# Attention and bilinear FFN on one core: the first batch's loads in phases, and five output transposes moved from TensorE to DMA

## The chip, the core and the metric

The kernel runs on one core of a Trainium2 chip. The metric is device time in microseconds (us) of one execution. Engines are named as the profile names them: PE is TensorE (matrix products and transposes), DVE is VectorE, ACT is ScalarE, POOL is GpSimd, SP is SyncE. DMAs are issued by a queue of SP or ACT ("hardware" queues in the profile) or by POOL ("software"); the profile counts the time of all of them against the same 16 DMA engines.

## The reference, cut to what matters

```python
B, H, S, D = 8, 8, 576, 64               # batches, heads, sequence, head size
scores = q @ k.transpose(0, 1, 3, 2) / sqrt(D) + bias_table[bucket(|i - j|)]   # 32 buckets per head
attn   = softmax(scores)
x      = (attn @ v)  -> (B*S, H*D) = (4608, 512)
out    = ((x @ w_a) * (x @ w_b)) @ w_out        # w_a, w_b: 512 x 1536, w_out: 1536 x 512
```

All inputs and the output are float32. The kernel takes its products of bfloat16 tiles, with float32 sums in PSUM; only the first transposes, of pairs 0 to 2 and of the first tails, read float32.

## The kernel before

The kernel works on 32 pairs of heads, four pairs to a batch. For each pair it multiplies q by k (`qk`), takes the exponential on ACT (`ex`, tile `at`), multiplies by the exponential of the bias on DVE (`mul`, tile `W`), multiplies by the values on PE (`av`), divides on DVE (`norm`, tile `XG`), and transposes the result into `xn` (`t_x`), the input of the FFN. From pair 4 on, FFN units (`pa`, `pb`, `po`) of an earlier batch are woven between the steps of attention, and PE is then the limit. Pairs 0 to 3 have no FFN work beside them. I call the stretch from the start to pair 8 the ramp.

The order of instructions is fixed by the program, and in the timelines here the sync queue issues its DMAs in that order.

The loads of the first batch (cuts marked with `...`):

```python
load32(0, q, q32, (nc.sync, nc.sync));  load32(0, k, k32, (nc.scalar, nc.scalar))
load32(1, q, q32, (nc.sync, nc.sync));  load32(1, k, k32, (nc.sync, nc.sync))
...
load_pad(nc.sync, k, kt32, 0, 1)        # last 64 rows of k ("tails"), float32
load_pad(nc.sync, q, qt32, 0, 1)
...
pad(nc.gpsimd, vt[0][:, 0:4, :, :], Dh + 1)     # memsets of zero padding on POOL
ones(nc.gpsimd, vt[0][:, 0:4, :, :])
...
nc.sync.dma_start(out=tab.ap(), in_=tab_sb[0:H, :])   # exp(bias) table to DRAM, W is read from it
load32(2, q, q32, (nc.sync, nc.sync))
load32(2, k, k32, (nc.sync, nc.sync))
load_w(nc.sync, 0)
...                                     # Wt
load_w(nc.sync, 1)

load_vp(0, 0)                           # software loads from here: values of pair 0
load_vt(0, 1)                           # value tails of batch 0
load_p(q, qn, 0, 3);  load_p(k, kn, 0, 3)
load_vp(0, 1)
load_t(v, None, 0, 4, 8)                # values of heads 4 to 7
load_w_in(0)
...                                     # pads, tails, q and k of batch 1, w_a and w_b
```

The output of a pair. `XG` has two buffers, so pair p + 2 writes what pair p's transpose reads:

```python
XG = [wpool.tile([128, 5, 2, Dh], BF16, name=f"XG{i}") for i in range(2)]
XD = 8
def t_x(p, where=None):
    xg = XG[p % 2]
    if XD <= p < NP - 1:                # by DMA, on the sync queue
        nc.sync.dma_start_transpose(out=xn_sb[hp][:, main]..., in_=xg[:, 0:4, :, :]...)
        nc.sync.dma_start_transpose(out=xn_sb[hp][:, rest]..., in_=xg[0:64, 4, :, :]...)
        return
    ps = bank(where, BF16, f"trx{p}")   # else five transposes on PE; c_x copies them out of PSUM
    for jq in range(5):
        nc.tensor.transpose(ps[:, 128 * jq:128 * jq + 128], xg[:, jq, :, :], ident)
```

The transposes of q and k of batch 2 (`QTb`, `KTb`, and the tails `QTt`, `KTt`) are DMA transposes too and go by the same sync queue (`turns`), one in each of steps 5, 6 and 7. Their sources, the last parts of `w_a` and `w_b`, and the whole of `w_out` are software loads issued at step 2:

```python
if s == 2:
    load_w_in(3);  load_w_in(4);  load_w_in(5)
    load_t(q, qn, 2, 0, 8);  load_t(k, kn, 2, 0, 8)
    ...
    load_tails(2, 2)
    load_w_out()                        # one load of 1,536 KB, tile wo
...
# steps 5 to 31
if s > XD:
    steps += [lambda: t_x(s - 1), lambda: turns(s)]
...
if s <= XD:
    steps += [lambda: t_x(s - 1, TR), lambda: c_x(s - 1), lambda: turns(s)]
```

The softmax here doesn't subtract the row's maximum and nothing guards it: scores larger than these inputs give would overflow.

## Time and profile before

The time before is 433.4 us, the median of 3 runs (432.4 to 433.4). The profiled execution spans 432.3 us; that execution took 434.11 us, more than the timed runs of its round, so a delta against it flatters the other kernel by about 0.7 us.

| from the profile of before | value |
|---|---|
| PE busy over the span | 411.5 us, 95% |
| PE busy, 100 to 400 us | 297.84 of 300 us |
| PE clock granted, 10.4 to 13.5 and 13.5 to 21.6 us | 0.72 and 0.50 |
| first `av` product with the main values on PE | 21.6 us |
| first FFN product leaves PSUM (`ha`) | 39.85 us |
| exponential of pair 8 starts | 82.29 us |

The window view of before shows where time can be won. Columns: stretch and its length, busy time of each engine with instruction counts, PE's granted clock, DMA share (time of the packets over the time of 16 engines; above 1 where packets overlap), GB/s. The engines stand in the order PE, PE's weight loads, DVE, ACT, POOL.

```profile
10.40:13.50 3.10, 0.38 (x1) 0.16 (x2) 0.38 (x1) 1.25 (x2) 2.89 (x5) 0.72 2.26 153
13.50:21.60 8.10, 6.88 (x30) 3.61 (x31) 2.53 (x8) 4.50 (x6) 7.51 (x13) 0.50 1.69 200
83.00:90.00 7.00, 6.84 (x81) 4.17 (x80) 3.39 (x9) 4.79 (x7) 6.02 (x8) 1.00 2.38 171
100.00:400.00 300.00, 297.84 (x2347) 144.94 (x2384) 133.54 (x313) 172.39 (x246) 42.89 (x52) 1.00 0.77 80
```

The last row says that PE has nothing to gain after 100 us except by doing less. In the first row PE works 0.38 of 3.1 us, and in the second its clock is at half: the short idle stretch is paid twice. The Trainium skill, "TensorE: Matmul & The Clock Gate", Part 1, puts the fall to half after an idle window of about 3.4 us. The trace agrees that half clock goes with a gap, but not on its length: PE's longest idle pieces here are 1.32 and 1.45 us, and a mean clock of 0.72 over 10.4 to 13.5 us puts the fall (1.00 to 0.50) at about 11.8 us, when PE had been idle since 10.37.

What PE and DVE wait for at the start, from the waits view of before (columns: total us, times, longest us):

```profile
PE trt L556 <- DMA qt<-in_q_dram: 1.5, 1, 1.5
PE trt L556 <- DMA kt<-in_k_dram: 1.3, 1, 1.3
DVE at L358 <- DMA W<-bias_tab: 4.2, 1, 4.2
```

And the chain that ended last, in order of time (start us, length us, what), has the same load in it:

```profile
1.17 3.97 DMA k<-in_k_dram
7.27 6.10 DMA qt<-in_q_dram
13.51 0.89 PE trt L556 x3
```

So the last of the float32 tails (of q) arrives at 13.4 us, after 6.1 us under way, and PE stands still for the tails of k and of q. Later in the ramp, the sync queue of before issues the batch-2 transposes with nothing between them (timeline view of SP; start us, time in the queue, what):

```profile
54.81 3.78 SPq L331 DMA_TRANSPOSE QTb<-qn  x1
58.77 9.02 SPq L331 DMA_TRANSPOSE KTb<-kn  x1
67.95 1.51 SPq L326 DMA_TRANSPOSE QTt<-qtl  x1
69.58 2.52 SPq L326 DMA_TRANSPOSE KTt<-ktl  x1
```

### The profile page before, as it was taken

To read this page: it belongs to the slowest core of one execution; us is meant where nothing else is said; L and a number is where in the kernel's file an instruction comes from. 1 tells how busy PE (TensorE), PEld (TensorE's weight loads), DVE (VectorE), ACT (ScalarE), POOL (GpSimd) and SP (SyncE) were. 2 spreads that over 40 slices of the span, in tenths; PEclk is the share of its full clock that TensorE was granted. 3 is DMA by queue.
4 is the path that set the end of the run, shared out by engine and by line. 5 is a ranking of instruction groups with operands and counts; after the bars stand their busy time and mean duration, and the time that the engine had idled before them with its cause. 6 is when DMAs were issued, how large, how long until landed. Compare 5 with 4: busy or idle time off the path is not lost.

```text
span 432.3 us, 8313 instructions
## 1 busy us (share of the span) xinstructions
PE 411.5 (95%) x3296; PEld 204.4 (47%) x3350; DVE 195.9 (45%) x482; ACT 241.4 (56%) x340; POOL 118.1 (27%) x164
## 2 busy tenths in 40 slices
PE   6688898999999999999999999999999999999995
PEld 2355444554445544444444454544444454444442
DVE  4295556545553455245634553355435541321320
ACT  4484766666665766666656675666566633223321
POOL 8989792583008100930073003000000000000000
PEclk9599999999999999999999999999999999999999
DMA  9999999999909990999099908931021002002004
GB/s 152 191 181 164 181 170 177 144 161 153 107 15 128 165 129 14 107 185 141 15 76 185 159 16 52 177 71 27 21 80 39 15 23 78 0 11 87 0 2 97
DMA packets 174055, 42.13 MB, mean 97 GB/s; under 512 B 160568, under 2 KB 169408, under 8 KB 174016
## 3 DMA queue, kind: packets, MB, share of 16 engines
q0 software_dynamic: 113296, 17.97, 67.4%
q1 hardware_dynamic: 59520, 23.27, 30.6%
q8 instruction: 26, 0.43, 0.4%
q10 hardware_dynamic: 1200, 0.36, 0.4%
q14 instruction: 13, 0.11, 0.1%
HBM read 38.83 MB, written 9.45 MB: 112 GB/s over the span
## 4 chain that ended last, share of the span: by engine, by line
PE 90%; DVE 3%; DMA 2%; ACT 2%; issue 1%; SPq 0%; ACTq 0%; DVEq 0%
PE pb L474 23%; PE po L484 22%; PE pa L464 21%; PE av L409 9%; PE qk L339 7%; PE av L400 2%; PE qkt L364 2%; PE qkt L367 1%; DMA qt<-in_q_dram 1%; DMA k<-in_k_dram 1%; DVE XG L418 1%; ACT at L350 1%; DVE at L358 1%; DVE g L477 1%; PE qktt L370 0%
## 5 line engine op out<-in xcount | busy, mean ns | idle before, releaser
L350 ACT ACTIVATE at<-qk 128x1024 bf16<-128x1024 f32 x128 | 125.9, 1024 | 23.5 <-PE qk L339 23.5
L477 DVE TENSOR_TENSOR g<-pb,ha 128x512 bf16<-128x512 f32 x108 | 74.7, 692 | 126.0 <-PE pb L474 102.7
L464 PE MATMUL pa<-xn,wa 128*128 128x512 bf16 x415 | 109.8, 379 | 0.8
L474 PE MATMUL pb<-xn,wb 128*128 128x512 bf16 x414 | 109.4, 379 | 1.0 <-DVE g L477 0.2
L468 ACT ACTIVATE ha<-pa 128x512 f32<-128x512 f32 x108 | 64.6, 598 | 77.2 <-PE pa L464 75.1
L484 PE MATMUL po<-wo,g 128*128 128x512 bf16 x416 | 99.6, 379 | 1.0 <-issue 0.2
L358 DVE TENSOR_TENSOR at<-at,W 128x512 bf16<-128x512 bf16 (+1 forms) x128 | 60.2, 483 | 14.2 <-ACT at L350 10.0
L474 PEld LDWEIGHTS <-wb 128*128 128x128 bf16 x432 | 38.6, 97 | 53.1 <-issue 18.0
L464 PEld LDWEIGHTS <-wa 128*128 128x128 bf16 x432 | 38.8, 98 | 49.3 <-issue 10.3
L484 PEld LDWEIGHTS <-g 128*128 128x128 bf16 x432 | 38.5, 98 | 46.1 <-issue 7.6
L488 ACT ACTIVATE ob<-po 128x512 f32<-128x512 f32 x36 | 21.5, 597 | 69.0 <-PE po L484 69.0
L124 POOL DMA_DIRECT2D vm<-in_v_dram x32 | 27.6, 876 | 112.0 <-PE av L409 111.8
L409 PE MATMUL av<-vm,at 128*128 128x65 bf16 x1024 | 47.3, 194 | 0.0
L409 PEld LDWEIGHTS <-at 128*128 128x128 bf16 x1024 | 42.7, 98 | 6.7
L417 DVE RECIPROCAL rc<-av 128x6 f32<-128x6 f32 x64 | 12.1, 188 | 53.4 <-PE av L409 53.4
L400 PE MATMUL av<-vt,att 128*128 128x130 bf16 x160 | 35.2, 220 | 0.1
L418 DVE TENSOR_TENSOR XG<-av,rc 128x384 bf16<-128x384 f32 x64 | 31.4, 491 | 2.9 <-DVE rc L417 0.8
L378 ACT ACTIVATE att<-qkt 128x1024 bf16<-128x1024 f32 x32 | 32.7, 1021 | 0.0
L339 PE MATMUL qk<-QTb,KTb 64*128 64x512 bf16 x192 | 29.1, 381 | 0.0
L124 POOL DMA_DIRECT2D qn<-in_q_dram x28 | 24.8, 914 | 12.9 <-PE qk L339 5.8
L124 POOL DMA_DIRECT2D kn<-in_k_dram x28 | 24.7, 900 | 13.0 <-DMA vt<-in_v_dram 4.6
L400 PEld LDWEIGHTS <-att 128*128 128x128 bf16 x160 | 15.8, 99 | 7.3 <-issue 0.7
(98 smaller groups left out, 214.5 us busy)
## 6 DMA issues: line engine op xcount, KB each, us to landing
out_dram<-ob SPq DMA_DIRECT2D x32, 256.0 KB, 4.3
qn<-in_q_dram POOLq DMA_DIRECT2D x28, 128.0 KB, 9.5
kn<-in_k_dram POOLq DMA_DIRECT2D x28, 128.0 KB, 13.1
vm<-in_v_dram POOLq DMA_DIRECT2D x28, 128.0 KB, 6.0
wa<-in_moe_w_a_dram POOLq DMA_DIRECT2D x6, 256.0 KB, 7.5
wb<-in_moe_w_b_dram POOLq DMA_DIRECT2D x6, 256.0 KB, 8.1
wo<-in_moe_w_out_dram POOLq DMA_DIRECT2D x1, 1536.0 KB, 15.4
out_dram<-ob SPq DMA_DIRECT2D x8, 128.0 KB, 2.3
```

Source lines behind the costliest of these rows:

```text
L124: nc.gpsimd.dma_start(out=(vm[b % 2][:, h0:h1, t, 0:Dh] if dst is None else dst[b % 2][:, :].rearrange("p (t h d) -> p t h d", h=H, t=NM)[ ...
L339: nc.tensor.matmul(out=ps[:, hh, :], lhsT=kT_(p, t)[r, :], rhs=qT[r, :, :], start=True, stop=True)
L350: nc.scalar.activation(out=at[:, :, :], in_=ps[:, :, :], func=ACTF.Exp, scale=scale)
L358: nc.vector.tensor_tensor(out=at[:, :, lo:hi], in0=at[:, :, lo:hi], in1=w[:, :, y:(None if z < 0 else z):-1], op=MULT)
L400: nc.tensor.matmul(out=pav[:, slot, :, :], lhsT=x, rhs=vt[b // 2 % 2][:, 4 * i + hp, :, :], start=True, stop=True)
L409: nc.tensor.matmul(out=pav[:, slot, hh, :], lhsT=x, rhs=vm[i][:, 2 * hp + hh, t, :], start=False, stop=True, skip_group_check=True)
L418: nc.vector.tensor_tensor(out=xg[:, j0:j0 + n, :, :], in0=pav[:, 0:n, :, 0:Dh], in1=rc.unsqueeze(3).to_broadcast([128, n, 2, Dh]), op=MULT)
L464: nc.tensor.matmul(out=pa[:, :], lhsT=wa_sb[df // FW][:, mc, 128 * (df % FW):128 * (df % FW) + 128], rhs=xn_sb[mc][:, xin(c)], start=(mc = ...
L468: nc.scalar.activation(out=ha[:, :], in_=pa[:, :], func=ACTF.Copy)
L474: nc.tensor.matmul(out=pb[:, :], lhsT=wb_sb[df // FW][:, mc, 128 * (df % FW):128 * (df % FW) + 128], rhs=xn_sb[mc][:, xin(c)], start=(mc = ...
L477: nc.vector.tensor_tensor(out=g_sb[df][:, :], in0=pb[:, :], in1=ff["ha"][:, :], op=MULT)
L484: nc.tensor.matmul(out=po[:, :], lhsT=g_sb[df][:, 128 * tt:128 * tt + 128], rhs=wo_sb[:, df, :], start=(df == 0), stop=(df == NDF - 1))
```

## The change

The intent has two halves. First, the loads of batch 0 come in phases: POOL does all its pads before its first value load, so that the float32 loads of the hardware queues have the DMA engines to themselves, and the values then come in a few large software loads. The loads of pair 2's keys move behind those of `W`. Second, the outputs of pairs 0, 1 and 4 to 6 are transposed by DMA as those from pair 8 on already were, which takes 25 transposes from PE and their copies from DVE.

```diff
-    load_pad(nc.sync, k, kt32, 0, 1)
+    load_pad(nc.scalar, k, kt32, 0, 1)
...
-    pad(nc.gpsimd, vt[0][:, 0:4, :, :], Dh + 1)
-    ones(nc.gpsimd, vt[0][:, 0:4, :, :])
     for i in range(2):
...
+        pad(nc.gpsimd, vt[i], Dh + 1)
+        ones(nc.gpsimd, vt[i])
+        for x in (ktl, qtl):
+            pad(nc.gpsimd, x[i], Dh)          # the later pads of these tiles are taken away
...
-    warm_up(1)
+    warm_up(2)
...
     load32(2, q, q32, (nc.sync, nc.sync))
-    load32(2, k, k32, (nc.sync, nc.sync))
     load_w(nc.sync, 0)
     ...                                       # Wt
+    load32(2, k, k32, (nc.sync, nc.sync))
     load_w(nc.sync, 1)
 
-    load_vp(0, 0)
+    load_v(0)                                 # all 8 heads, four loads
     load_vt(0, 1)
     load_p(q, qn, 0, 3)
     load_p(k, kn, 0, 3)
-    load_vp(0, 1)
-    load_t(v, None, 0, 4, 8)
...
-    XD = 8
+    XD = {0, 1, 4, 5, 6} | set(range(8, NP - 1))
...
-        if XD <= p < NP - 1:
+        if p in XD:
...                                            # in the loop of pairs 0 to 3
-        if s > 1:
-            t_x(s - 2, FF)
...
-        if s > 1:
-            c_x(s - 2)
...
-            tails_next(s + 1, 1, None)
+            tails_next(s + 1, 1, ACT)
...
+        if s in (1, 2):
+            t_x(s - 1)
...                                            # pairs 5 to 31
-            if s > XD:
+            if s - 1 in XD:
                 steps += [lambda: t_x(s - 1), lambda: turns(s)]
```

The second `warm_up` product is one more that PE does without use before the first transposes. Two more moves are cut: `av(s - 1, 4)` goes ahead of `mul(s, 2)`, and the copy of pair 2's output goes to ACT. Where pair 4 to 6's outputs go by DMA, their transposes are now put into the sync queue ahead of the batch-2 transposes of the same step.

More of the change, by code (lines that the diff above doesn't have):

```diff
@@ L235 @@
     load_p(k, kn, 0, 3)
-    load_vp(0, 1)
-    load_t(v, None, 0, 4, 8)
     load_w_in(0)
-    for x in (ktl, qtl):
-        pad(nc.gpsimd, x[0][:, 4:8, :, :], Dh)
     load_tails(1, 1)
@@ L244 @@
     load_w_in(1)
-    pad(nc.gpsimd, vt[0][:, 4:8, :, :], Dh + 1)
-    ones(nc.gpsimd, vt[0][:, 4:8, :, :])
     load_vt(1, 1)
@@ L446, in c_x @@
         b, hp = divmod(p, 4)
-        if XD <= p < NP - 1:
+        if p in XD:
             return
@@ L599 @@
         ex_tail(s)
+        if s > 0:
+            av(s - 1, 4)
         mul(s, 2)
         if s > 0:
-            av(s - 1, 4)
             norm(s - 1, 3)
+        if s in (1, 2):
+            t_x(s - 1)
         if s < 3:
@@ L611 @@
             load_t(k, kn, 2, 0, 8)
-            for x in (ktl, qtl):
-                pad(nc.gpsimd, x[1], Dh)
             load_tails(2, 2)
@@ L637 @@
         if s == 4:
-            steps += [lambda: mul(3, 3), lambda: mul_tail(3), lambda: t_x(2, FF), lambda: c_x(2),
+            steps += [lambda: mul(3, 3), lambda: mul_tail(3), lambda: t_x(2, FF), lambda: c_x(2, ACT),
                       A(0, 1, 2), N(0), A(3, 4), N(3), lambda: t_x(3, FF), lambda: c_x(3), U,
@@ L659 @@
                       lambda: qk_tail(s), lambda: ex_tail(s), U]
-            if s <= XD:
+            if s - 1 not in XD:
                 steps += [lambda: t_x(s - 1, TR), lambda: c_x(s - 1), lambda: turns(s)]
@@ L678 @@
         if s == 4:
-            pad(nc.gpsimd, vt[1], Dh + 1)
-            ones(nc.gpsimd, vt[1])
-            for x in (ktl, qtl):
-                pad(nc.gpsimd, x[0][:, 0:4, :, :], Dh)
+            pass
         if new and s % 4 == 2 and b + 1 < B:
```

## The prediction

> **What bounds it now.** By the table of windows, TensorE (PE) is busy 99% of 100-400 us at full clock; only PE work itself could be saved there. The loss is in the ramp: from 0 to 70 us PE is idle 13.6 us, and its granted clock is 0.72 in 10.4-13.5 us and 0.50 in 13.5-21.6 us. A start-up gain moves the whole span one for one.
>
> The chain of waits shows the ramp: load of k to 5.1 us, the tail loads' issues (the queue waits 0.7 us), then 6.1 us of `qt<-q` landing, until 13.37 us; the tail transposes (`trt`) run at 13.51. PE is nearly empty for 3.1 us before, and the clock falls to half. The Trainium skill ("TensorE: Matmul & The Clock Gate", Part 1) says an idle window of about 3.4 us does that; this trace agrees. Next, `at<-at,W` waits 4.2 us for W (landing ~19.3 us), and the first attention-times-values product (`av`) runs at 21.3 us. From 21.6 to 35 us DVE is 88% and ACT 84% busy.
>
> **What the change does.**
> 1. HW loads first. GpSimd does all pads before its first value load: at the trace's 0.52-0.54 us per large memset about 7.4 us, so value loads begin near 9.4 us instead of 3.5. Until then the float32 loads have the 16 DMA engines alone (skill, "DMA: Bandwidth & Descriptors", Issuing engines are not separate DMA queues: all share them). kt goes out on ACT's queue near 2.3 us, qt near 6.5; landing should take about 4 us (as first loads do) instead of 6: tails at 10.5-11 us, 2.5-3 us earlier, PE gap almost closed, clock kept, another 1.5-2 us. W lands near 15-16 us.
> 2. Price: values of all 8 heads arrive in four loads that the first `av` needs whole, plus vt behind them: issued 9.4-14.2 us, landed about 19 (18-20.5). The first `av`, otherwise possible near 17, becomes bound by values: about 19.3 us. Pair 3's q/k follow, about 22.5, needed about then. So about 2 us of the possible 4-5 survive.
> 3. Outputs of pairs 0, 1, 4, 5, 6 by DMA: 25 PE transposes go (5 of one pair take 0.34 + 0.29 us, some overlapped) and 5 x 0.5 us of DVE copies; two tail copies (0.42 us) and one output copy (0.5) move to ACT. In 21.6-35 us that is some 1.9 us less on the busiest engine, of which about 1 us shows, because ACT (+0.8) is nearly as busy. PE work in 40-70 us falls about 1 us. DMA transposes land in 3.3 us, up to 8 under load; XG is reused two steps later, so no wait expected.
>
> **Sum.** First `av` -2, second stage -1, pairs 4-6 and step 4 about -1.3: -4.3 us. Steady state unchanged.
>
> Predicted 429.1 us (-1.0%), 8 in 10 within 425.8 to 432.4. Faster by over 2%: 0.06; within 2%: 0.92; slower by over 2%: 0.02.
>
> **What would show it.** 1: `trt` at 10.5-11 us, no half-clock stretch at 13-20. 2: PE idle before the first `av`, ended by DMA of vm or vt, near 19. 3: `trx` 20 instead of 45, `xn<-XG` transposes 56 instead of 46; DVE under 85% in that stage; first `pa` near 35.5-36 us instead of 38.76. Windows beyond 100 us alike.
>
> **What would make it wrong.** If the ACT queue has to wait before issuing kt, the exp of the bias table (4.83 us) slips and all after it. If values land beyond 21 us, the ramp gains nothing and the clock may fall in that gap. If they land by 17, the gain is about 6 us. Later q/k/weight loads, about 2 us late, could stall pair 4.

## The result, and the profile after

The kernel after takes 444.47 us (median of 4 runs, 442.78 to 445.85) against 433.43 us (4 runs, 432.38 to 433.67) for the kernel before. The ratio is 1.0258, with a 95% interval of 1.0215 to 1.0300: slower by 2.6%. The profiled executions span 432.3 us before and 442.0 us after.

To see where the 9.7 us of the profiled span came from, I took the start of the first exponential of each pair (ACT) and the first write of `XG` of each pair (DVE) from both traces. "Delta" is after minus before, in us.

| event | before | after | delta |
|---|---|---|---|
| first tail of k transposed on PE (`trt`) | 11.69 | 11.72 | +0.03 |
| first tail of q transposed on PE (`trt`) | 13.51 | 11.88 | -1.63 |
| exp of pair 1 | 17.11 | 14.62 | -2.49 |
| exp of pair 2 | 24.06 | 27.80 | +3.74 |
| `XG` of pair 0 written | 24.41 | 27.15 | +2.74 |
| `XG` of pair 3 written | 37.47 | 41.84 | +4.37 |
| exp of pair 4 | 42.88 | 49.09 | +6.21 |
| exp of pair 7 | 73.47 | 79.13 | +5.65 |
| exp of pair 8 | 82.29 | 90.73 | +8.44 |
| exp of pair 9 | 91.11 | 100.38 | +9.27 |
| exp of pair 31 | 339.38 | 348.67 | +9.29 |

The 9.3 us are all lost before pair 9, in three places: 2.7 us by the first `XG`, 3.5 us more by pair 4, and 3.6 us more from pair 7 to pair 9. Between pairs 4 and 7 half a microsecond is won back. From pair 9 on the two kernels run alike.

The last tails landed at 9.74 us (13.38 before), but PE reached them only at 11.72. It was still busy with pairs 0 and 1, because in this profile its clock rose later: the first record of full clock is at 10.36 us (before: 4.95), and the first four `qk` products took 1.33 us instead of 0.85 (timelines of before and after):

```profile
7.45 0.85 PE L339 MATMUL qk<-QT,KT 64*128 64x512 bf16 x4 [0.19 <-DVE QT L257]
8.24 1.33 PE L335 MATMUL qk<-QT,KT 64*128 64x512 bf16 x4
```

The waits view of after names a DMA in each place. The line numbers differ from before because lines were moved.

```profile
PE trk L511 <- DMA k<-in_k_dram: 4.8, 1, 4.8
PE av L396 <- DMA vt<-in_v_dram: 1.0, 1, 1.0
DVE XG L414 <- DMA xn<-XG: 2.2, 2, 1.7
PE qk L335 <- DMA KTb<-kn: 3.2, 1, 3.2
PE qkt L363 <- DMA KTt<-ktl: 0.5, 1, 0.5
```

The waits for `qt` and `kt` of before are gone, so the first step of the change did what it should. In their place PE waits 4.8 us for pair 2's keys and then 1.0 us for the value tails. `XG` of a later pair waits for a DMA that still reads it. Pair 8 waits for its transposed keys.

The pieces of the chain of after that hold a DMA:

```profile
13.45 10.53 DMA vt<-in_v_dram
35.13 7.72 DMA xn<-XG
67.83 20.20 DMA vm<-in_v_dram
88.03 9.32 DMA KTt<-ktl
```

The value tails were issued at 13.45 us and took 10.5 us; a pair's output transpose took 7.7 us. The windows of after show what PE lost:

```profile
13.50:21.60 8.10, 2.39 (x17) 1.48 (x14) 2.70 (x8) 3.89 (x5) 4.34 (x7) 0.73 1.89 158
21.60:26.00 4.40, 3.42 (x29) 2.05 (x28) 1.50 (x4) 1.30 (x2) 2.28 (x4) 0.50 1.59 170
38.80:47.30 8.50, 5.93 (x71) 4.03 (x70) 2.69 (x10) 1.80 (x4) 5.56 (x8) 0.83 2.08 162
83.00:90.00 7.00, 4.13 (x25) 1.86 (x23) 2.57 (x7) 3.58 (x5) 2.09 (x3) 1.00 1.86 135
100.00:400.00 300.00, 300.00 (x2431) 145.78 (x2428) 135.68 (x320) 176.27 (x250) 52.06 (x63) 1.00 0.88 86
```

The half-clock stretch was not removed but moved: it was 13.5 to 21.6 us, and a window of 18 to 26 us of after shows 0.50, behind a longer gap (4.8 us). A second, shorter one lies in 38.8 to 47.3 us (mean 0.83). In 83 to 90 us PE worked 4.13 of 7 us where before it worked 6.84.

The sync queue of after, over the time of the batch-2 transposes:

```profile
62.39 1.22 SPq L432 DMA_TRANSPOSE xn<-XG  x1
63.85 4.54 SPq L327 DMA_TRANSPOSE QTb<-qn  x1
72.38 1.19 SPq L429 DMA_TRANSPOSE xn<-XG  x1
73.62 1.98 SPq L432 DMA_TRANSPOSE xn<-XG  x1
75.78 6.77 SPq L327 DMA_TRANSPOSE KTb<-kn  x1
83.25 1.22 SPq L429 DMA_TRANSPOSE xn<-XG  x1
84.52 1.22 SPq L432 DMA_TRANSPOSE xn<-XG  x1
85.90 2.03 SPq L322 DMA_TRANSPOSE QTt<-qtl  x1
88.03 1.28 SPq L322 DMA_TRANSPOSE KTt<-ktl  x1
```

Each batch-2 transpose now stands behind an output transpose (`xn<-XG`), which can only be issued when its `XG` is written. `KTb` is issued at 75.78 us instead of 58.77, `KTt` at 88.03 instead of 69.58, and pair 8 begins at 90.7.

### The profile page after: what moved, and what is told of

It is laid out like the page before. It is cut to its first block, busy times and chain, and to the rows that moved or that the text cites. A ratio compares the mean times of both kernels' runs of the same rounds, so it can differ in the third digit from the quotient of the medians.

```text
span 442.0 us, 8320 instructions
## 1 busy us (share of the span) xinstructions
PE 415.8 (94%) x3326; PEld 205.1 (46%) x3326; DVE 192.8 (44%) x468; ACT 242.8 (55%) x344; POOL 114.9 (26%) x152
## 4 chain that ended last, share of the span: by engine, by line
PE 82%; DMA 11%; POOL 3%; DVE 1%; ACT 1%; issue 1%; SPq 0%; DVEq 0%; POOLq 0%
PE pb L470 22%; PE pa L460 20%; PE po L480 20%; PE av L405 8%; PE qk L335 6%; DMA vm<-in_v_dram 5%; DMA vt<-in_v_dram 2%; DMA KTt<-ktl 2%; PE av L396 2%; DMA xn<-XG 2%; PE qkt L363 1%; PE qkt L360 1%; POOL vm L124 1%; ACT at L346 1%; PE qktt L366 0%
## 5 line engine op out<-in xcount | busy, mean ns | idle before, releaser
L470 PE MATMUL pb<-xn,wb 128*128 128x512 bf16 x432 | 111.8, 381 | 0.0
L460 PE MATMUL pa<-xn,wa 128*128 128x512 bf16 x432 | 111.4, 380 | 0.0
L480 PE MATMUL po<-wo,g 128*128 128x512 bf16 x432 | 102.4, 379 | 0.0
```

The lines of the kernel that those rows point to most:

```text
L460: nc.tensor.matmul(out=pa[:, :], lhsT=wa_sb[df // FW][:, mc, 128 * (df % FW):128 * (df % FW) + 128], rhs=xn_sb[mc][:, xin(c)], start=(mc = ...
L470: nc.tensor.matmul(out=pb[:, :], lhsT=wb_sb[df // FW][:, mc, 128 * (df % FW):128 * (df % FW) + 128], rhs=xn_sb[mc][:, xin(c)], start=(mc = ...
L480: nc.tensor.matmul(out=po[:, :], lhsT=g_sb[df][:, 128 * tt:128 * tt + 128], rhs=wo_sb[:, df, :], start=(df == 0), stop=(df == NDF - 1))
```

## The experiments

My theory after the comparison had three parts, one for each place: (A) the start is lost by order: pair 2's keys stand behind `W` and `Wt`, and the value tails behind four whole value loads; (B) the loss by pair 4 is the output transposes of pairs 0 and 1, through `XG`; (C) the loss at pair 8 is the order of the sync queue. The main rival was that some common cause, the late start of the software loads or the traffic of the added transposes on the DMA engines, makes everything late, so that mending one wait brings the next one. 18 kernels ran; all gave the reference's result. Deltas are again against the profile of before, and times are medians of the timed runs with their range.

### The parts of the theory, one at a time

**a1_k2_early**: part A, only the order of the float32 loads.

```diff
     load32(2, q, q32, (nc.sync, nc.sync))
+    load32(2, k, k32, (nc.sync, nc.sync))
     load_w(nc.sync, 0)
     ...
-    load32(2, k, k32, (nc.sync, nc.sync))
     load_w(nc.sync, 1)
```

> The changed kernel with one thing undone: the float32 keys of pair 2 are again issued before the loads of W. Theory A (the first attention-times-values product is bound by the landing of vt, issued late behind four large value loads): the 4.8 us wait of the transposes of k goes, but the first av still starts near 23.5-24 us, and the time stays within 1 us of the changed kernel's 444.5 (443.5-445). Theory B (the order of that key load is what delays the start): first av near 21 us, 441-442 us.

Measured: 442.74 us (441.45 to 443.54, 4 runs), ratio 1.0220 [1.0188, 1.0252]. The wait for the keys is gone, but another has its place (waits view):

```profile
PE av L396 <- DMA vt<-in_v_dram: 4.8, 1, 4.8
DVE XG L414 <- DMA xn<-XG: 3.3, 1, 3.3
```

The first `XG` comes 0.82 us later than before instead of 2.74, so 1.9 us were won there. At pair 3 the delta is +4.49 and at the exp of pair 4 +6.62, as large as after: in this profile the gain was used up in waiting for the output transpose. The first `av` comes at 22.20 us, between the two theories: both the keys and the value tails bind, one behind the other. The time is 1.7 us under that of after, but the intervals of the two ratios overlap.

**a2_pads_late**: the rival for the start. The pads go back to where they were, so that value loads begin at 2.9 us instead of 9.3; the order of the loads stays as after.

```diff
+    pad(nc.gpsimd, vt[0][:, 0:4, :, :], Dh + 1)
+    ones(nc.gpsimd, vt[0][:, 0:4, :, :])
     for i in range(2):
-        pad(nc.gpsimd, vt[i], Dh + 1)
-        ones(nc.gpsimd, vt[i])
-        for x in (ktl, qtl):
-            pad(nc.gpsimd, x[i], Dh)
...                                   # and the other pads at their old places
```

> The changed kernel with GpSimd's pads back at their old places, so that value loads start near 3.5 us instead of 9.3; their shape and order stay. Theory A (late start of the value loads): values and vt land by about 17-19 us, first av at 19-21.5 us instead of 24.1, time 441-442.5 us; tails of pair 0 land later, up to 13 us. Theory C (the large shape, all heads before the first av, is the cause whatever the start): first av still past 23 us, time unchanged at 444.

Measured: 445.86 us (444.49 to 447.93, 4 runs), ratio 1.0299 [1.0257, 1.0342]. It is no better, so theory A failed; by the profile `XG` of pair 0 is 3.74 us late. `W` is issued at 14.15 us instead of 9.73 and pair 2's keys at 15.86 instead of 11.44, and PE still waits 4.7 us for them. So the late start of the value loads, which the prediction had named as the price, is not what costs the start. Early large value loads only put the delay onto the float32 loads.

**a3_out01_pe**: part B. The outputs of pairs 0 and 1 go back to PE.

```diff
-    XD = {0, 1, 4, 5, 6} | set(range(8, NP - 1))
+    XD = {4, 5, 6} | set(range(8, NP - 1))
...                                   # t_x(s - 2, FF) and c_x(s - 2) restored for s > 1, t_x(s - 1) taken away
```

> The changed kernel with outputs of pairs 0 and 1 transposed by TensorE again, as before. Theory: the 7.7 us landing of the output transposes of pair 1 holds its XG buffer, norm of pair 3 waits 1.7 us for it, PE goes idle and its clock falls; without it the delay against the old kernel stays at about +2.7 us from the first av to the first FFN unit (now +2.7 growing to +6.2), time 441 us (440-442). Rival (no buffer wait, only ramp noise): 444.

Measured: 442.40 us (440.54 to 442.92, 4 runs), ratio 1.0203 [1.0163, 1.0243]. The wait of `XG` is gone and pair 4 is 2.94 us late instead of 6.21, as part B said. But pair 8 is 8.35 us late all the same. The 3.3 us were lost again: `w_out` took 22.0 us to land (15.4 in before), and PE waited 3.2 us for it (waits view):

```profile
PE po L480 <- DMA wo<-in_moe_w_out_dram: 3.2, 1, 3.2
```

**a4_turns_first**: part C. In steps 5 to 7 the batch-2 transposes go ahead of the output transposes.

```diff
             if s - 1 in XD:
-                steps += [lambda: t_x(s - 1), lambda: turns(s)]
+                steps += ([lambda: turns(s), lambda: t_x(s - 1)] if s < 8 else
+                          [lambda: t_x(s - 1), lambda: turns(s)])
```

> The changed kernel with the q, k and tail transposes of batch 2 put ahead of the output transposes of pairs 4 to 6 on the sync queue, same number of DMA transposes. Theory D (queue order: the sync queue waits for XG with the transpose of keys behind it, issued at 75.8 instead of 58.8 us): keys are transposed at least 4 us earlier, the 3.2 us wait of PE for KTb near 87-90 us goes, time 441 us (440-442). Rival E (the extra DMA traffic itself is too much): the wait stays and so does the time, 444.

Measured: 438.14 us (437.89 to 438.73, 4 runs), ratio 1.0119 [1.0092, 1.0146]. `KTb` is issued at 68.80 us instead of 75.78 and PE waits 0.9 us for it instead of 3.2 (timeline of SP, waits view):

```profile
68.80 8.11 SPq L327 DMA_TRANSPOSE KTb<-kn  x1
PE qk L335 <- DMA KTb<-kn: 0.9, 1, 0.9
```

The step from pair 7 to pair 8 costs 0.5 us (delta +2.46 to +3.00) instead of 2.8. So the order of the queue is a cause, and shown. The whole gain is 6.3 us by the medians, and all four runs lie at least 4 us under the fastest of after. This profile puts only 2.5 us of that behind pair 7; the rest is in the ramp up to pair 4, whose code is the same as after and which was only about 3 us late and not 6.2. Why is not shown. The ramp of the same code differs between profiles (the first `XG` came at +1.26 here and at +2.74 in after), so differences of 1 to 2 us in a single profile of the start prove little by themselves.

### Is it the buffer, or the traffic?

**c1_xg_four**: four buffers of `XG` instead of two, so that no pair of the ramp waits for a transpose to have read it.

```diff
-    XG = [... for i in range(2)]
+    XG = [... for i in range(4)]
...
-        xg = XG[p % 2]
+        xg = XG[p % 4]
```

> The changed kernel with four buffers for XG instead of two, so no norm has to wait for an output transpose; everything else the same. If only the buffer reuse costs: no wait of the norm for xn<-XG, delay at the first FFN unit back to about +2.9 us, time 441 us (440-442). If the late landing itself costs (the first FFN unit needs the transposed outputs of pair 1, landed near 42.9 us, buffer or not): the wait moves from DVE to the first pa, 0-1.5 us return, time 443-444.5.

Measured: 444.77 us (444.14 to 446.65, 4 runs), ratio 1.0262 [1.0236, 1.0288], the same as after. The waits view:

```profile
PE trk L511 <- DMA k<-in_k_dram: 5.1, 1, 5.1
PE po L480 <- DMA wo<-in_moe_w_out_dram: 5.0, 1, 5.0
PE pa L460 <- DMA xn<-XG: 1.2, 1, 1.2
```

The wait of `XG` is gone and pair 4 is only 3.06 us late, but then PE waits 5.0 us for `w_out`, which takes 22.8 us to land, and pair 8 is 10.14 us late. So the reuse of the buffer was a place where the delay appeared, and removing it alone gains nothing: the loss appeared again at a weight whose load the diff does not touch. It does not follow that the traffic is the cause, because the order of the sync queue is still that of after here; a4, which mends that order and nothing else, has no such wait. Four buffers together with the mended order were not run.

**d4_before_outputs**: the kernel before with only the second half of the change, the outputs by DMA.

```diff
-    XD = 8
+    XD = {0, 1, 4, 5, 6} | set(range(8, NP - 1))
...                                   # t_x, c_x, av(s - 1, 4) and the copy of pair 2 as in the change; loads as before
```

> The other half alone: the old kernel with its start untouched (loads, pads, values as before), and only the outputs of pairs 0, 1, 4, 5, 6 transposed by DMA as in the change. Theory (the output half loses by itself, through XG waiting for a slow transpose and keys queued behind output transposes): no delay at the first av, then +1.5 to +3.5 us at step 4 and +3 us more at pair 8: 437-440 us. Rival (everything is lost in the start, the output half is a small gain as predicted): 431-433 us.

Measured: 440.59 us (439.74 to 440.97, 4 runs), ratio 1.0159 [1.0144, 1.0174]: 6.9 us slower by the medians (440.59 against 433.66). The first `XG` is as early as before (+0.42), `XG` then waits 3.9 us for `xn<-XG` (longest 2.8), pair 4 is 3.94 us late, and the wait for `KTb` (1.7 us) brings it to 5.25.

**e0_start_only**: the first half alone, on the kernel after with the outputs of pairs 0 to 7 by PE.

```diff
-    XD = {0, 1, 4, 5, 6} | set(range(8, NP - 1))
+    XD = set(range(8, NP - 1))
...                                   # and t_x, c_x of pairs 0 and 1 restored
```

> The start half alone: all outputs of pairs 0 to 7 by TensorE as in the old kernel, the start as in the change (pads first, four whole value loads, keys of pair 2 behind W, tail copies on ACT). If the two halves add up to the whole 11 us (the output half alone cost 6.9), this is about 437.5 (436-439). If they overlap, more: 440 or above; if the output half makes the start's lateness worse, less: 434.5-436.

Measured: 435.92 us (435.54 to 437.42, 4 runs), ratio 1.0070 [1.0042, 1.0099]: 2.5 us slower (against 433.41). PE waits 6.6 us for float32 keys (in two waits, the longest 6.3), the first `XG` is 1.41 us late, and that delta then stays the same to the end (+1.48 at pair 31). The halves cost 2.5 and 6.9 us, 9.4 together, against 11.0 measured. The missing 1.6 us are either interaction or the scatter of the ramp; the runs do not tell.

The traces count what the added transposes do to the packets of the loads. These are the DMA packets that started in a stretch of the profiled execution, counted from the records of the packets; "long" are packets of over 0.4 us, and the last column is their summed time over 16 engines.

```
kernel                 software packets, 20-40 us   long packets, 20-50 us   their time / 16, us
outputs of pairs 0 and 1 by PE:
before                          16,336                        7                     0.3
c4_front_out_turns              16,248                        8                     0.4
e0_start_only                   15,886                        8                     0.3
c2_out_pe_turns                 13,972                        4                     0.2
a3_out01_pe                     13,562                       24                     0.9
outputs of pairs 0 and 1 by DMA:
c1_xg_four                      13,336                       71                     4.7
after                           13,210                      106                     4.3
a4_turns_first                  13,177                      194                    11.2
c3_front                        12,666                      149                     9.0
d4_before_outputs               11,156                      149                    11.8
```

The long packets tell the two groups apart: 4 to 24 without output transposes in that stretch, 71 to 194 with them. Most of the long ones are packets of the software loads (76 of the 106 in after, 121 of the 149 in d4). The number of software packets alone does not: a3 and c2, without these transposes, have hardly more than after. In single microseconds it is plainer. In before at 28 to 31 us the software loads run at 1,165 to 1,228 packets a microsecond with hardly any hardware packet beside them. In d4_before_outputs, whose pair-0 and pair-1 output transposes were issued from 26.4 to 31.8 us, only 96 and 74 software packets started in the microseconds at 29 and 30, and one packet took 2.27 us. Why packets take so long beside these transposes is not settled: the records show that they do, and not what holds them.

### Mending all of it

**c2_out_pe_turns**: a3 and a4 together (outputs 0 and 1 by PE, batch-2 transposes first). The start stays as after.

```diff
-    XD = {0, 1, 4, 5, 6} | set(range(8, NP - 1))
+    XD = {4, 5, 6} | set(range(8, NP - 1))
...
+                steps += ([lambda: turns(s), lambda: t_x(s - 1)] if s < 8 else
```

> Both single repairs together: outputs of pairs 0 and 1 by TensorE, and the q, k and tail transposes of batch 2 ahead of the output transposes. If the two losses are separate and add: about +2.7 us from the start alone, less 0.5: 436 us (435-437.5). If the run with only the first repair lost its gain again at 80-88 us because loads are late in general (there PE waited 3.2 us for wo), some of that comes back here too: 438-440.

Measured: 435.94 us (434.74 to 436.99, 4 runs), ratio 1.0050 [1.0029, 1.0071], as expected. Only the wait for pair 2's keys is left of the three (5.9 us in this profile), and pair 31 is 2.7 us late.

With after, a3 and a4 this run makes a square, and the square weighs the parts. The order of the sync queue is worth 6.3 us with the outputs of pairs 0 and 1 by DMA (after to a4) and 6.5 us without (a3 to c2); those outputs are worth 2.1 and 2.2 us. (These are differences of medians; the times of before in the rounds differ by 0.5 us.) So the order is the largest single loss. From a3 to c2 nothing but the order changes: `w_out` lands in 16.0 us instead of 22.0, PE does not wait for it, and from pair 7 to pair 9 the profile loses nothing (-0.3 us) where a3 loses 6.0. Part of these 6.0 us is the clock: after its wait of 3.2 us PE ran at 0.50 from 83.0 to 89.9 us. And c2, which transposes the outputs of pairs 4 to 6 by DMA, takes as long as e0 (435.92 us), which does not: with this start they cost nothing that can be measured once they stand in the right order. How the order delays the landing of `w_out` is not shown.

**c3_front**: the start alone mended: keys of pair 2 ahead of `W`, and the values in the old order (pair 0, value tails, q and k of pair 3, the rest). Pads stay first.

```diff
     load32(2, q, q32, (nc.sync, nc.sync))
+    load32(2, k, k32, (nc.sync, nc.sync))
...
-    load_v(0)
+    load_vp(0, 0)
     load_vt(0, 1)
     load_p(q, qn, 0, 3)
     load_p(k, kn, 0, 3)
+    load_vp(0, 1)
+    load_t(v, None, 0, 4, 8)
```

> The changed kernel with only its start mended: keys of pair 2 before the W loads, and after the pads the values in the old order (the two heads of pair 0, vt, pair 3's q and k, then the rest in smaller loads). Theory: the first av needs 1536 rows instead of 4608 after 9.3 us and starts near 18-19.5 us, 2 us before the old kernel; of that the waits for output transposes and for the transposed keys, which are left, take part back: 438-441 us. Rival (value loads are not what binds): first av stays past 21.5 us, 442 or more.

Measured: 439.00 us (438.10 to 440.51, 4 runs), ratio 1.0115 [1.0098, 1.0132]. The first `XG` comes 4.41 us earlier than before and that of pair 1 5.41 us earlier. So the hardware-first start is worth what the prediction called possible (4 to 5 us), and the order of the loads behind it undid it. After that `XG` waits 2.3 us for output transposes, pair 4 is only 1.42 us early, and PE waits 6.2 us for `w_out`: pair 8 is 5.82 us late.

**c4_front_out_turns**: c2 and c3 together, all three places mended.

> All three mended: start as in the run before, outputs of pairs 0 and 1 by TensorE, and batch 2's transposes ahead of the output transposes of pairs 4 to 6. Theory (three separate losses, the rest of the change is a gain): first av at 18-19.5 us, no wait for XG, none above 1 us for KTb: 429-432 us, below the old kernel's 433.4. Rival (late software loads cost elsewhere): 433-437.

Measured: 433.59 us (433.22 to 434.44, 4 runs), ratio 1.0000 [0.9985, 1.0015]. The 11 us are gone. The 429 to 432 us hoped for were missed. The clock of PE is full from 9 to 77 us, pair 4 starts 3.64 us earlier than before and pair 7 4.20 us earlier, and then all of it is lost in one step; pair 8 starts 0.16 us late. The chain of c4 says why:

```profile
58.82 18.12 DMA wo<-in_moe_w_out_dram
```

In before `w_out` is issued at 57.37 us and takes 15.4 us, so it lands at about 72.8 us, and the first product that reads it is at 78.2 us. With a ramp that is 4.2 us faster it is wanted at about 74, and it lands at 76.9 us. PE waits 2.8 us for it, and then runs at half clock (windows view), so that the step costs 4.4 us:

```profile
77.20:80.50 3.30, 3.30 (x14) 1.56 (x13) 0.00 (x0) 0.77 (x2) 1.32 (x2) 0.50 1.61 158
```

### Where the last four microseconds went

**d1_wo_early**: c4 with `w_out` loaded ahead of q and k of batch 2.

```diff
     load_w_in(5)
+    load_w_out()
     load_t(q, qn, 2, 0, 8)
     load_t(k, kn, 2, 0, 8)
     load_tails(2, 2)
-    load_w_out()
```

> The kernel with all three repairs, and the one load of wo (1.5 MB) moved ahead of the q and k loads of batch 2 on the software queue. In the run without this the lead over the old kernel was 4.2 us at the exp of pair 7 and was gone at pair 8, where PE waited 2.8 us for wo. If that wait is the whole of what was given back: no wait for wo, 429.5 us (428.5-430.8). If the queue is simply full, so that something else lands late instead (keys of batch 2, its values): 432-434.

Measured: 440.47 us (439.52 to 441.63, 4 runs), ratio 1.0160 [1.0139, 1.0181]: much worse. The waits view:

```profile
DVE XG L416 <- DMA xn<-XG: 8.0, 2, 6.6
PE qktt L368 <- DVE XG L416: 5.4, 1, 5.4
PE qk L337 <- DMA KTb<-kn: 1.4, 1, 1.4
```

`w_out` is no longer waited for. But `QTb`, whose source is now behind it, is issued only at 66.12 us, the output transpose of pair 4 behind that at 70.42, and `XG` of pair 6 waits for it. The software stream is full, and what is moved forward makes something else late.

**d2_wo_early_out_pe**: d1 with the outputs of pairs 4 to 6 on PE (`XD = set(range(8, NP - 1))`), to see whether the sync queue is the whole of d1's loss.

> As the run with the early wo, but the outputs of pairs 4 to 6 too by TensorE, so that of the change only its start (mended) and the copies moved to ACT are left. If output transposes by DMA are a gain once the queue's order is right: 0.5 to 1 us slower than with them, 430-431.5. If their traffic and their place in the queue still cost: faster than with them, 428-429.5.

Measured: 437.71 us (436.04 to 438.62, 6 runs), ratio 1.0091 [1.0073, 1.0109]. Not the whole: the wait of `XG` is gone, and PE waits 4.3 us for `KTb`.

**d3_before_wo_early**: the control, the same move of `load_w_out()` in the kernel before.

> Control: the old kernel with only wo loaded earlier. Its trace shows no wait of PE for wo, so nothing should come of it: within 1 us of 433.4, or up to 1 us slower because q and k of batch 2 land later.

Measured: 433.47 us (433.30 to 434.28, 4 runs), ratio 1.0003 [0.9987, 1.0020]. In the slower ramp the order of these loads does not matter.

**e1_loads_early** and **e2_pads_few**: c4 with the pads later, so that the software stream as a whole begins sooner. In e1 the pads are back at their old places (as in a2, loads from 3.5 us). In e2 only the pads of `vt[0]` come first:

```diff
     for i in range(2):
...
-        pad(nc.gpsimd, vt[i], Dh + 1)
-        ones(nc.gpsimd, vt[i])
-        for x in (ktl, qtl):
-            pad(nc.gpsimd, x[i], Dh)
+        if i == 0:
+            pad(nc.gpsimd, vt[0], Dh + 1)
+            ones(nc.gpsimd, vt[0])
```

> As the run with all three repairs, but GpSimd's pads at the old places too, so the software queue is not empty from 3.5 to 9.3 us. If that idle time of the software queue is what made wo late (landed 77 us against 72.8 in the old kernel, PE waited 2.8 us): wo lands by about 74 us, the tails of pair 0 and W land later than with pads first, and the sum is 431.5-434. If wo still lands at 77 or later, the start of the software loads is not the reason, and the time is 434-436.

> As the run with all three repairs, but only the pads of the first vt come before the values, so software loads start near 3.5-4 us with the mended HW order, the other pads later in between. Same question as with all pads late: wo landed by 74-75 us and 431-433.5 us if the idle software queue was the reason; 434 or more if the early software loads delay the float32 loads as in the run with large value loads.

Measured: e1 432.23 us (432.14 to 432.43, 4 runs), ratio 0.9980 [0.9957, 1.0002]; e2 432.50 us (431.58 to 433.50, 4 runs), ratio 0.9986 [0.9958, 1.0014]. The start gains less (pair 4 at -1.61 and -0.60 us) but nothing is waited for at pair 8: `w_out` is issued at 58.27 and 56.85 us and takes 15.4 and 15.1 us. At the exp of pair 31 the profiles are 2.14 and 1.41 us ahead. Both intervals still hold 1.

**e3_wo_three**: c4 with `w_out` in three loads of 512 KB, so that its first product would not need all of it.

```diff
-        nc.gpsimd.dma_start(out=wo_sb[:, :, :], in_=moe_w_out.rearrange("(t p) n -> p t n", p=128))
+        for i in range(3):
+            nc.gpsimd.dma_start(
+                out=wo_sb[:, 4 * i:4 * i + 4, :],
+                in_=moe_w_out[512 * i:512 * i + 512, :].rearrange("(t p) n -> p t n", p=128))
```

> The run with all three repairs, with wo loaded in three thirds in order of their use instead of one load, at the same place. If PE there waited only because one semaphore stands for all of 1.5 MB: the first third lands 8 us or more before 77, no wait, time 430-431.5 us. If the queues are simply behind in general: the wait goes over to the keys of batch 2 (KTb) or its values, 432.5-434.

Measured: 436.54 us (434.33 to 438.13, 4 runs), ratio 1.0061 [1.0016, 1.0107]. PE's wait for `w_out` falls to 1.0 us, but `XG` now waits 4.8 us for an output transpose and PE 2.6 us for `KTb`. As in d1, the wait moved.

**f1_early_out_pe** and **f2_front_out_pe**: no output transposes by DMA before pair 8. f1 is e1 with `XD = set(range(8, NP - 1))`. f2 is c4 with the same, built from the kernel before:

```diff
-    load_pad(nc.sync, k, kt32, 0, 1)
+    load_pad(nc.scalar, k, kt32, 0, 1)
...                                   # all pads before the first value load, as in the change
-    warm_up(1)
+    warm_up(2)
...                                   # order of loads as before; outputs of pairs 0 to 7 by PE as before
-            tails_next(s + 1, 1, None)
+            tails_next(s + 1, 1, ACT)
```

together with the moves of `av(s - 1, 4)` and of pair 2's copies to ACT that the change has.

> As the run with all repairs and early software loads, but no output transposes by DMA before pair 8, so only kt on ACT's queue and three copies on ACT are left of the change. That run was 1.6 us ahead of the old kernel at pair 4 and gained 0.6 more by pair 8. If the output transposes of pairs 4 to 6, rightly placed, are worth those 0.6 us: 432.3-433 us here. If they cost: 431-431.8.

> The old kernel with pads first, kt on ACT's queue and three copies on ACT; loads in the old order, no output transposes by DMA before pair 8. With those transposes (the run with all three repairs) the lead of 4.2 us at pair 7 was lost to wo landing at 77 us. If output transposes sharing the DMA engines with wo and the keys made wo late: wo lands near 74.5 us, PE waits for it under 0.5 us, and 2.5-3.5 us are kept: 430-431.5 us. If the late start of the software loads alone makes wo late: a wait of 2 us or more, 432.5-434.

Measured in the same rounds: f1 433.40 us (432.70 to 433.87, 5 runs), ratio 0.9994 [0.9980, 1.0007]; f2 **431.81 us** (431.59 to 432.66, 5 runs), ratio 0.9957 [0.9945, 0.9970], before in these rounds 433.68 us (433.20 to 434.53, 9 runs). f2 beats both kernels, by 1.9 us and by about 12.7 us (the latter by medians of different rounds). Its chain shows `w_out` again, issued at 59.66 us and landing at 75.97:

```profile
59.66 16.30 DMA wo<-in_moe_w_out_dram
```

f2 is 3.91 us ahead at pair 7 and 2.22 us at pair 8; PE waits 1.5 us for `w_out`, where in c4 it was 2.8. So the loss of c4 at that step was of both kinds. About 2 us of it went with the last three output transposes (c4 is at +0.16 at pair 31, f2 at -2.2): the wait is 1.3 us shorter, and no half-clock stretch follows it. The rest goes with the later start of the software stream (f1 and e1, which start it at 3.5 us, do not wait for `w_out`, but they also win less at the start and so want it later: pair 4 at -1.46 and -1.61 us). The four kernels c4, f2, e1 and f1 do not add up simply: taking the transposes away helped where pads come first, and e1 and f1 cannot be told apart.

## Why the prediction was wrong

It was 429.1 us with a range up to 432.4, and the kernel takes 444.5. The sum was -2, -1 and -1.3 us. Measured in the profile, the same three stretches are +2.7, +3.5 and -0.6, and a fourth, which the sum did not have, is +3.6.

1. **Hardware loads first: right.** `kt` was issued on ACT's queue at 2.34 us (predicted 2.3), the pads kept POOL until 9.34 us (predicted 9.4), the last tails landed at 9.74 us and were transposed at 11.72 (predicted 10.5 to 11; PE's late clock held them up), and the exp of pair 1 came 2.5 us earlier. c3 and c4 show that the start (with its second `warm_up` product and the copies on ACT) is worth about 4 us at the first `XG` when the rest is in order.

2. **The price: wrong, and this was the first step to fail.** The prediction had the values "landed about 19 (18-20.5)" and the first `av` at 19.3 us. The last value tails landed at 23.98 us (13.45 and 10.53 in the chain) and the first `av` ran at 24.12. The size that failed was the rate of the software loads beside hardware loads. The values and their tails are 576 KB in packets of 128 bytes, 4,608 packets. Between 12 and 22 us the trace of after starts 501 software packets a microsecond, and about 220 hardware packets beside them, where software alone ran at 1,200 in before (28 to 31 us). The mixed rate could be read before the change: in the same stretch before has 461 and 303. At 501 they take 9.2 us, which from 12 us on is beyond 21 us even with nothing else in the software stream, where the prediction allowed until 19. The page on DMA that it cited says that all share the same engines; it had used this for the hardware loads only, and not for the value loads against `W`, `Wt` and the keys.

   The prediction also missed a wait altogether: it named the values and pair 3, but not the keys of pair 2, which the diff moves behind `W` and `Wt`. PE waited 4.8 us for them. Its own condition, "If values land beyond 21 us, the ramp gains nothing and the clock may fall in that gap", is what happened. a1 shows that both bind; a2 shows that the late start itself is not the cause; c3 shows that the order is.

3. **Outputs by DMA: the saving was right in kind, "no wait expected" was wrong.** The counts came as said (20 `trx` instead of 45, 56 `xn<-XG`), and DVE was busy 62% in 21.6 to 35 us (8.32 of 13.4 us). But that stretch was no longer bound by DVE, and the first `pa` came at 43.5 us instead of 35.5 to 36. The argument held its own contradiction: transposes that land in "up to 8" us, and a buffer reused two steps later, when two steps in that stretch are 7.8 us (first writes of `XG` at 29.66 and 37.47 us in before) and the transpose is issued only after the last write. The measured landing was 7.7 us. Beyond that, c1 shows that removing this wait alone gains nothing: the loss came back at `w_out`, whose load the diff does not touch. The square of after, a3, a4 and c2 puts 2.1 to 2.2 us on the outputs of pairs 0 and 1. That their traffic slows the loads beside them fits the long packets (0.3 us of the 16 engines' time in before, 4.3 in after and 11.8 in d4), but how much of the 2 us is traffic and how much the buffer is not taken apart.

4. **The order of the sync queue: missing.** This was the largest loss. The prediction costed the added transposes as work, and not as places in a queue that waits in order; "no wait expected" looked at `XG` alone. The timeline of SP of before shows that queue; the prediction did not use it. a4 shows the cost: between pairs 7 and 8 the loss fell from 2.8 to 0.5 us with the order alone, and the time by 6.3 us (6.5 from a3 to c2). That is more than the 3.6 us that the profile of after loses from pair 7 to pair 9; where the rest comes from is open.

5. **Steady state unchanged: right.** The delta is +9.27 at pair 9 and +9.29 at pair 31.

What stays open: what makes single packets take up to 2.3 us beside an output transpose; how the order of the sync queue delays `w_out`; why the start of the same code varies by 1.5 us and more between profiles; and the 1.6 us by which the two halves fall short of the whole. One part of the second question the traces do answer. Six profiles have the same first instructions (a3, e0, c2, a4, c1, after). Their first record of full PE clock comes at 4.5, 4.6, 8.6, 8.8, 9.6 and 10.4 us, and the tails are transposed at 10.04, 10.22, 11.20, 11.27, 11.32 and 11.72 us, in the same order. The first `XG` does not follow that order, so this is not all of it.

## What to carry to other kernels

When a change moves loads or puts work on DMA, list for each queue what stands behind the moved item and when that is first read; a transfer that "has time" can still hold back one that has not. Take the rate of a load from a stretch of the trace with the same neighbours, not from one where it ran alone, and test a suspected buffer by doubling it: if the time stays and the wait appears elsewhere, the cause is not the buffer alone. Then mend the suspects in pairs: here the order of the queue was weighed only when it was mended with and without the other repair. A gain early in a ramp is kept only until the first load that is already just in time, here `w_out`, so look up the slack of the next few loads before counting it.

## What the Trainium skill lacked or had wrong

- "DMA: Bandwidth & Descriptors", Issuing engines are not separate DMA queues, says that the DMAs of all engines share the 16 DMA engines and interleave. The runs agree and give the size that it lacks: software loads of 128-byte packets ran at 1,165 to 1,228 packets a microsecond alone and at 501 beside hardware loads (after, 12 to 22 us).
- The same page, Rules for kernel authors, says that a DMA transpose next to ordinary DMAs "needs nothing". That is about correctness, and no run here gave a wrong result. Of time it says nothing: beside the output transposes software packets fell to 74 and 96 a microsecond (d4_before_outputs, 29 to 31 us), and packets over 0.4 us rose from 7 to 149.
- "Advanced Engine Details and Errata", X-Bar Transpose (TRN2), says that transposes are as fast as regular DMAs. For the transfer itself the trace of after agrees roughly: an output transpose landed in 5.6 us in the median, a 128 KB value load in 7.5. I found no page that tells what they cost the loads beside them: with them the packets over 0.4 us took 11.8 us of the 16 engines' time in d4_before_outputs (20 to 50 us), without them 0.3 in before.
- "TensorE: Matmul & The Clock Gate", Part 1, fits in kind: after a gap of 4.8 us the clock was 0.50 at 21.6 to 26 us, and in c4_front_out_turns, which has no such gap in the first 60 us, it was 1.00 there. As a limit its window of about 3.4 us does not show: the clock fell with a gap of 2.8 us in c4_front_out_turns (0.50 at 77.2 to 80.5 us), and it did not fall with one of 3.2 us in after (1.00 at 87.1 to 90.3 and at 90.3 to 97 us).
- No page that I found warns that a DMA that waits for its source in an engine's queue holds back those behind it: `KTb` was issued at 75.78 us instead of 58.77.
